# Attention with an MLP gate: one tile's statistics on ScalarE, normalization on VectorE, dummy products in the prologue, more half-unit scores

## The chip, the cores and the metric

The kernel runs on one core of a Trainium2 chip. The metric is device time in microseconds (us) of one execution; a profiled span is about 2 us shorter than the time of the same run. Each ratio compares runs on the same chip from the same batch. Single profiles can come from different chips, and their details vary by a few us between executions (the changed kernel's first exponential starts at 14.64 us in one profile and at 13.81 in another). Each experiment was timed five or six times beside eleven runs of the kernel before, and has a ratio with a 95% interval. A ratio is the mean time of one kernel's fast runs over that of the other's fast runs of the same rounds, so it is not quite the ratio of the medians quoted beside it.

## The reference, cut to what matters

```python
x  = A_x                                    # 1 x 2048 x 1024, bf16
xn = layernorm(x)                           # no learned scale or shift
# A: attention with 32 heads of 32, on xn
q, k, v = split(xn @ wqkv)
p = softmax(q @ k.T * 32 ** -0.5)           # 32 heads x 2048 x 2048 exponentials
s = merge_heads(p @ v) @ wo
# B: an MLP on xn, which normalizes once more
h = gelu_tanh(layernorm(xn) @ w1 + b1)      # hidden size 3584
g = silu(h @ w2 + b2)
out = x + s * g
```

The 134 million exponentials are ScalarE's work: 1024 instructions of 128x1024. Everything before the first of them is the prologue: load a token tile (128 tokens), take its mean and variance, normalize, transpose, project to K, Q and V.

## The kernel before, in the parts that matter

A small planner in the kernel lists all operations with estimated durations and dependencies, simulates the engines, and fixes the order of the instructions of each engine. Constants at the top steer it; a changed estimate can therefore reorder instructions anywhere. One *unit* is four heads, 256 queries and 256 keys: eight score products, two exponentials, and the P·V products. A Q block is 256 queries, and eight units (one for each pair of token tiles as keys) make up one block's row. Q products are made for 512 queries at a time; what is called Q block 1 below is the second of these, and the first unit that needs it is unit 16.

The prologue normalizes tiles and transposes them by DMA from tile 2 on; GpSimd normalizes all tiles that are not in `DN`:

```python
DN = (2, 3)
XA, XB, XW = 8, 5, 9
...
    for t in (lo, lo + 1):
        if t in DN:
            xnop[t] = dve(lambda e, t=t: e.tensor_scalar(xnb[t % 4], xst[t], mv[:, t, 0:1], lnp[:, t, 1:2],
                          op0=ALU.subtract, op1=ALU.mult), 360, [XS(t), ("mv", t), ("rs", n)], [("xnb", t % 4)], 0.5)
            continue
        xnop[t] = pool(lambda e, t=t: e.tensor_scalar(xnb[t % 4], xst[t], lnp[:, t, 1:2], lnp[:, t, 5:6], ...
    for t in (lo, lo + 1):
        ...
            add("SP", lambda e, t=t: e.dma_start_transpose(out=xnT[:, :, t * 128:(t + 1) * 128], in_=xnb[t % 4]),
                1290, 0, [("xnb", t % 4)], ...)
    pro_q.append(k_pair_item(n, False))
```

SyncE issues every transfer, in one queue (158.12 of the 160.16 MB that the page counts; the rest is listed as instructions): the transposes, and also the first MLP weights, of which the first product starts only at 65.29 us. The first w1 loads are held back to certain tiles by an extra dependency (the last argument); the w2 loads are not held back by tiles at all:

```python
def load_w1(p):
    ...
        dma(f"w1{gi}{i}", lambda e, i=i, src=src: e.dma_start(w1r[gi][:, 4 * i:4 * i + 4], src), 332000, [], [("w1", gi, i)], 3,
            [xnop[XW + 2 * p]] if p < 3 else [])

def load_w2(q, r):
    ...
    src = B_w2[r * 7 * 128:(r + 1) * 7 * 128, q * 256:(q + 1) * 256].rearrange("(f p) n -> p f n", p=128)
    dma(f"w2{i}", lambda e: e.dma_start(w2r[:, i], src), 580000, [], [("w2", i)])
```

Scores of the first `NARROW` = 16 units are issued in halves of two heads, so that an exponential can start after four products:

```python
if u < NARROW:
    for h in range(2):
        plan.s_queue.append(add("PE", lambda e, h=h: s_fn(e, (2 * h, 2 * h + 1)), 232.0, TL + 30, R, [("S", pr[h])], mode="r"))
else:
    plan.s_queue.append(add("PE", lambda e: s_fn(e, range(4)), 235.0, TL + 30, R, [("S", pr[0]), ("S", pr[1])], mode="r"))
```

The softmax here doesn't subtract the row's maximum and nothing guards it: scores larger than these inputs give would overflow.

## Time and profile before

| | before |
|---|---|
| time, median (range) | 1057.43 us (1055.95 to 1057.48), 3 runs |
| profiled span | 1055.8 us |
| ScalarE: start of first exponential | 15.25 us |
| ScalarE: gaps from there until it never waits again | 19.15 us |
| ScalarE: from the end of the last exponential to the end | 14.15 us |

ScalarE is busy without a break in the middle (930.00 of 930.00 us between 100 and 1030), so the last three rows are where time can be won: an earlier first exponential, smaller gaps after it, a shorter tail. The lines they are read from stand in the prediction. Columns: start, duration of issuing, queue, line, kind, out<-in, number of issues.

```profile
36.35 1.93 SPq L933 DMA_DIRECT2D w1r<-in_B_w_dram  x2
38.33 0.51 SPq L940 DMA_DIRECT2D w2r<-in_B_w_dram  x1
38.88 3.98 SPq L894 DMA_TRANSPOSE big<-gw  x2
```

### The profile page before, as it was taken

What the parts mean: (1) busy time and instruction counts of PE and PEld (TensorE: products, weight loads), DVE (VectorE), ACT (ScalarE), POOL (GpSimd) and SP (SyncE); (2) the same over time, 40 slices, a digit from 0 to 9 for tenths busy, and PEclk for the clock granted to TensorE, in tenths of its full rate; (3) what the DMA queues carried; (4) which work ended last, traced back from release to release, by engine and by line L of the source; (5) the groups of instructions that cost most, each with busy time, mean ns of one, the idle gap of its engine ahead of it and who ended that gap; (6) DMA issues with size and microseconds to landing.
All of it is one profiled execution on the core that took longest, in us unless ns stands there. A gap on an engine that the chain in (4) does not pass through costs nothing.

```text
span 1055.8 us, 31978 instructions
## 1 busy us (share of the span) xinstructions
PE 1024.0 (97%) x14230; PEld 632.8 (60%) x14230; DVE 967.9 (92%) x1463; ACT 1010.3 (96%) x1100; POOL 28.6 (3%) x40
## 2 busy tenths in 40 slices
PE   7998999999999999999999999999999999899997
PEld 4565457656666566656765666556665566564442
DVE  7579899999999989999999999999899999978997
ACT  2779999999999999999999999999999999999994
POOL 3600000000000000000000000000000000000000
PEclk8999999999999999999999999999999999999999
DMA  8955256634275446633565556433664687663322
GB/s 219 232 153 156 56 144 198 184 97 117 86 219 155 135 139 188 166 89 100 160 177 143 146 159 190 135 90 99 179 196 141 192 238 206 193 195 111 124 88 71
DMA packets 302371, 160.16 MB, mean 152 GB/s; under 512 B 40218, under 2 KB 293146, under 8 KB 302234
## 3 DMA queue, kind: packets, MB, share of 16 engines
q1 hardware_dynamic: 302234, 158.12, 53.3%
q8 instruction: 112, 1.84, 0.7%
q14 instruction: 25, 0.20, 0.1%
HBM read 142.35 MB, written 12.06 MB: 146 GB/s over the span
## 4 chain that ended last, share of the span: by engine, by line
ACT 88%; PE 7%; DMA 2%; DVE 2%; SPq 0%; POOL 0%; issue 0%; DVEq 0%; POOLq 0%
ACT P L1134 82%; ACT ut L995 5%; PE ps L701 5%; ACT gw L1031 1%; PE ps L696 1%; PE ps L1120 1%; DMA big<-yT 1%; DMA hT<-in_A_x_dram 1%; DVE ut L854 0%; DMA big<-gw 0%; DVE w1r L1281 0%; DVE V L771 0%; SPq L715 0%; POOL gw L886 0%; SPq L723 0%
## 5 line engine op out<-in xcount | busy, mean ns | idle before, releaser
L1134 ACT ACTIVATE P<-ps 128x1024 bf16<-128x1024 f32 x1024 | 965.3, 1245 | 23.4 <-PE ps L1120 23.3
L1164 DVE TENSOR_TENSOR PA<-P 128x2048 bf16<-128x2048 bf16 x246 | 298.7, 1216 | 15.8 <-ACT P L1134 15.1
L701 PE MATMUL ps<-yT,w1r 128*128 128x256 bf16 x1792 | 231.4, 274 | 3.4 <-DVE nv L1217 1.6
L701 PE MATMUL ps<-w2r,hT 128*128 128x256 bf16 x1792 | 227.2, 274 | 1.6 <-DVE hT L998 0.9
L701 PEld LDWEIGHTS ps<-yT,w1r 128*128 128x128 bf16 x1792 | 162.5, 98 | 58.9 <-issue 30.2
L701 PEld LDWEIGHTS ps<-w2r,hT 128*128 128x128 bf16 x1792 | 162.2, 98 | 53.0 <-issue 31.2
L696 PE MATMUL ps<-P,V 128*32 128x256 bf16 x4096 | 146.5, 274 | 0.0
L1169 DVE TENSOR_TENSOR PA<-PA 128x1024 bf16<-128x1024 bf16 x204 | 138.2, 681 | 1.5
L701 PE MATMUL ps<-big,qk 128*128 128x512 bf16 (+2 forms) x568 | 134.6, 368 | 1.5 <-DMA big<-gw 0.8
L701 PE MATMUL ps<-qk,big 128*128 128x256 bf16 (+1 forms) x736 | 127.3, 306 | 3.2 <-DMA big<-gw 2.7
L696 PEld LDWEIGHTS ps<-P,V 128*32 128x32 bf16 x4096 | 96.5, 96 | 35.6 <-issue 22.6
L1120 PE MATMUL ps<-qk 32*128 32x256 bf16 x2048 | 106.0, 273 | 8.6 <-ACT P L1134 7.6
L1120 PE MATMUL ps<-QKT 32*128 32x256 bf16 x2048 | 101.7, 273 | 2.7 <-ACT P L1134 2.3
L701 PEld LDWEIGHTS ps<-qk,big 128*128 128x128 bf16 x736 | 64.9, 98 | 45.0 <-issue 17.7
L701 PEld LDWEIGHTS ps<-big,qk 128*128 128x128 bf16 x568 | 50.5, 102 | 52.6 <-issue 16.0
L980 DVE TENSOR_TENSOR xb<-ps,b1T 128x512 bf16<-128x512 f32 x112 | 76.4, 685 | 4.7 <-PE ps L701 4.0
L1120 PEld LDWEIGHTS ps<-qk 32*128 32x128 bf16 x2048 | 31.6, 92 | 75.9 <-ACT P L1134 71.6
L1120 PEld LDWEIGHTS ps<-QKT 32*128 32x128 bf16 x2048 | 30.3, 92 | 71.5 <-ACT P L1134 68.5
L995 ACT ACTIVATE ut<-ut 128x1024 f32<-128x1024 f32 x56 | 72.5, 1295 | 0.0
L998 DVE SCALAR_TENSOR_TENSOR hT<-ut,xb 128x1024 bf16<-128x1024 f32 x56 | 67.9, 1212 | 1.3 <-ACT ut L995 1.0
L993 DVE SCALAR_TENSOR_TENSOR ut<-hT,xb 128x1024 f32<-128x1024 bf16 x56 | 68.0, 1214 | 0.0
L696 PE MATMUL ps<-PA,ones 128*32 128x256 bf16 x896 | 46.4, 275 | 0.0
(79 smaller groups left out, 529.7 us busy)
## 6 DMA issues: line engine op xcount, KB each, us to landing
w1r<-in_B_w_dram SPq DMA_DIRECT2D x224, 256.0 KB, 3.5
w2r<-in_B_w_dram SPq DMA_DIRECT2D x128, 448.0 KB, 4.3
qk<-in_A_wqkv_dram SPq DMA_DIRECT2D x16, 256.0 KB, 3.3
g_scratch<-gw SPq DMA_DIRECT2D x32, 128.0 KB, 3.6
o_scratch<-ot SPq DMA_DIRECT2D x56, 64.0 KB, 3.1
big<-o_scratch SPq DMA_DIRECT2D x28, 128.0 KB, 3.7
hT<-in_A_x_dram SPq DMA_DIRECT2D x10, 256.0 KB, 4.2
qk<-in_A_wqkv_dram SPq DMA_DIRECT2D x4, 512.0 KB, 3.7
```

The source lines that it names most:

```text
L696: ins = e.matmul(dst(j), lhsT=lhsT(j), rhs=rhs(j), start=start, stop=stop, tile_position=(0, 32 * j), skip_group_check=True)
L701: return e.matmul(dst, lhsT=lhsT, rhs=rhs, start=start, stop=stop, skip_group_check=True)
L980: dve(lambda e: e.tensor_tensor(xb_t[i2][:, p % 2].rearrange("p (k t) -> p k t", k=2), bank(it.bank).rearrange("p (k t) -> p k t", k=2), b ...
L993: dve(lambda e, r=r: e.scalar_tensor_tensor(ut_t[i2][:, r], h[:, r], 1.0 / GA, xb[:, r], op0=ALU.add, op1=ALU.mult), c_f32(r.stop - r.star ...
L995: act(lambda e: e.activation(ut_t[i2][:], ut_t[i2][:], ACT.Tanh, scale=GC * GA), c_acts(1024), [("ut", i2, 0), ("ut", i2, 1)], [("ut", i2, ...
L998: dve(lambda e, r=r: e.scalar_tensor_tensor(h[:, r], ut_t[i2][:, r], 1.0, xb[:, r], op0=ALU.add, op1=ALU.mult), c_f32(r.stop - r.start), [ ...
L1031: act(lambda e: e.activation(zh, z, ACT.Tanh, scale=0.5), c_acts(1024), [("z", 0), ("z", 1)], [("zh",)], 1)
L1120: ins = e.matmul(bank(b0[j], kk * 256, (kk + 1) * 256), lhsT=QKT[sl][32 * j:32 * j + 32, 1, kb * 128:(kb + 1) * 128], rhs=QKT[sl][32 * j:3 ...
L1134: x = act(lambda e, h=h: e.activation(P[pi][:, 2 * h:2 * h + 2].rearrange("p j k q -> p (j k q)"), ps[:, pr[h] * 1024:(pr[h] + 1) * 1024], ...
L1164: add2.append(dve(lambda e, p0=p0, a0=a0: e.tensor_tensor(PA_all[:, a0:a0 + 2].rearrange("p u j q -> p (u j) q"), P_all[:, p0:p0 + 2, :, 0 ...
L1169: add4.append(dve(lambda e, a0=a0: e.tensor_tensor(PA[a0], PA[a0], PA[a0 + 1], op=ALU.add), c_b16(1024), [("PA", a0 + 1)], [("PA", a0)], P ...
```

## The change

It means to shorten the prologue: ScalarE takes the statistics of tile 2 (two passes with a summed output) in place of VectorE; VectorE normalizes every tile in place of GpSimd; dummy products fill TensorE's idle time up to 32 us, in the hope that its clock, granted at 0.50 from 10.20 to 13.62 and from 20.44 to 23.86 us in the kernel before, stays at 1.00; 22 instead of 16 units are scored in halves; a fourth token tile is loaded ahead of the Q/K weights (`XF`). Duration estimates and constants of the planner are corrected, which reorders the rest. Core of the diff (cuts marked):

```diff
-HARD = 45
+HARD = 48
-AGE_D = 2500
-HOLD = 500
+AGE_D = 3500
+HOLD = 400
-GRACE1 = 4000
+GRACE1 = 2500
-XF = 3
+XF = 4
-DN = (2, 3)
+DN = (2, 3, 4, 5, 6, 7, 8, 9, 10, 11, 12, 13, 14, 15)
-PART = 3
+PART = 4
+HALF = 1
+NU = 22
+AS = (2,)
+FILL = 300
 ...
             if best is None:
+                if self.fill and t < 32000 and nxt > t + FILL and (t > 6000 or not self.fill[0].left):
+                    bf = bank_for(t)
+                    if bf is not None and bf[0] <= t:
+                        it = self.fill.pop()
+                        best = (t, 3, it.chunks[0], (it, bf[1]))
 ...
-    NARROW = 16
-    plan.narrow = 2 * NARROW
+    NARROW = NU
+    plan.narrow = 2 * NARROW if HALF else NARROW
 ...
+                if t in AS:
+                    junk = yT[:, 4:8, :].rearrange("p c t -> p (c t)")
+                    act(lambda e, t=t: e.activation(junk, xst[t], ACT.Copy, scale=-1.0 / 32768, accum_out=lnp[:, t, 2:3]), ...)
+                    act(lambda e, t=t: e.activation(junk, xst[t], ACT.Square, bias=lnp[:, t, 2:3], scale=1.0 / 32,
+                                                    accum_out=mv[:, t, 1:2]), ...)
+                    dve(lambda e, t=t: e.tensor_scalar_mul(mv[:, t, 0:1], lnp[:, t, 2:3], -32.0), ...)
+                else:
                     ... (BN_STATS and BN_AGGR as before)
 ...
-            if u < NARROW:
+            if u < 16:          # sums of P by TensorE: the same units as before
```

More of the change, by code (lines that the diff above doesn't have):

```diff
@@ L43 @@
 NCUT = 2
+HALF = 1
+NU = 22
+QE = 0
+AS = (2,)
+FILL = 300
+ADJ2 = 0
 TD = 2
@@ L78, in __init__ @@
         self.skip = []
+        self.fill = []
         self.ring_last = {}
@@ L117, in units_of @@
     def units_of(self, s):
+        if not self.half:
+            return s
         return s // 2 if s < self.narrow else s - self.narrow // 2
@@ L129, in run @@
         state = {"mode": "c", "bw": 0.0, "s": 0, "pv": 0, "pvopen": [], "dopen": None, "susp": None,
-                 "done": 0.0, "last_bank": 7}
+                 "done": 0.0, "cend": 0.0, "last_bank": 7}
         bank_free = {b: [] for b in (4, 5, 6, 7)}
@@ L160, in commit @@
                 state["bw"] = max(state["bw"], t) + o.nbytes / 380.0
-                o.fin = state["bw"] + {"w1": WLAT, "w2": WLAT, "tp": 2400.0, "x0": 1900.0, "x1": 1900.0}.get(o.sem[:2], 2300.0)
+                o.fin = state["bw"] + {"w1": WLAT, "w2": WLAT, "tp": 2800.0, "x0": 2050.0, "x1": 2000.0, "x2": 2500.0}.get(o.sem[:2], 2300.0)
             else:
@@ L298, in pe_step @@
                 if o.left == 0:
-                    cands.append((o.ready, 1, o, None))
+                    late = state["mode"] == "f" and state["dopen"] is not None
+                    cands.append((max(o.ready, state["cend"]) + ADJ2 if late else o.ready, 1, o, None))
             if state["dopen"] is not None:
@@ L360, in pe_step @@
             if best is None:
+                if self.fill and t < 32000 and nxt > t + FILL and (t > 6000 or not self.fill[0].left):
[3 more added lines that the diff above has]
+                        best = (t, 3, it.chunks[0], (it, bf[1]))
+            if best is None:
                 if nxt < INF:
@@ L366, in pe_step @@
             if o.mode != state["mode"]:
-                start += 95.0
+                start += 105.0 if state["mode"] == "c" else 95.0
                 state["mode"] = o.mode
@@ L386, in pe_step @@
                     state["pv"] += 1
+                elif cls == 3:
+                    o.item.k = 1
                 else:
@@ L389, in pe_step @@
                     heads[opening[2]] += 1
-            if cls == 0:
+            if cls == 3:
+                pass
+            elif cls == 0:
                 state["s"] += 1
@@ L401, in pe_step @@
                 it.k += 1
+                if cls == 1:
+                    state["cend"] = start
                 if it.k == len(it.chunks):
@@ L437, in run @@
                 wake(max(t, soon[e][0][0]), e)
+        for it in self.fill:
+            it.chunks[0].dead = True
+            it.chunks[0].start = it.chunks[0].fin = 0.0
         left = [o for o in self.ops if o.start is None]
@@ L564, in bass_recurrent_scan__mha_block__mixer_channel_mlp__prompt_kernel @@
     plan = _Plan()
-    NARROW = 16
-    plan.narrow = 2 * NARROW
+    NARROW = NU
+    plan.narrow = 2 * NARROW if HALF else NARROW
+    plan.half = HALF
     WARM = 13
@@ L722, in load_qk @@
             src = A_wqkv[:, which * D + hg * 128: which * D + (hg + 1) * 128].rearrange("(c p) n -> p c n", p=128)
-            dma(f"wqk{i}", lambda e: e.dma_start(wqk[i], src), 262144 * 8 // 5, [], [("wqk", i)], 3,
+            dma(f"wqk{i}", lambda e: e.dma_start(wqk[i], src), 262144 * 2, [], [("wqk", i)], 3,
                 [xnop[NT - 1]] if nqk["n"] == 3 else [])
@@ L728, in load_v @@
             src = A_wqkv[:, 2 * D + pr * 256: 2 * D + (pr + 1) * 256].rearrange("(c p) n -> p c n", p=128)
-            dma("wv", lambda e: e.dma_start(wv, src), 665000, [], [("wv",)])
+            dma("wv", lambda e: e.dma_start(wv, src), 850000, [], [("wv",)])
         for t in range(XF):
@@ L809, in warm_item, with fill_item @@
             return it
+        def fill_item():
+            it = _Item("fill")
+            chunk(it, lambda e, b: full(e, bank(b), ident[:], ident[:].unsqueeze(1).to_broadcast([128, 4, 128]), True, True), Q512, [("ident",)])
+            return it
         def qk_tile_item(t):
@@ L850, in bass_recurrent_scan__mha_block__mixer_channel_mlp__prompt_kernel @@
         pro_q.append(warm_item())
+        plan.fill = [fill_item() for _ in range(80)]
         for n in range(NPR):
             for t in (2 * n, 2 * n + 1):
-                for c in range(2):
-                    dve(lambda e, t=t, c=c: e.bn_stats(stats[:, t, c, :], xst[t][:, c * 512:(c + 1) * 512]),
-                        600, [XS(t)], [("st", t, c)], 1)
-                dve(lambda e, t=t: e.bn_aggr(mv[:, t, :], stats[:, t, :, :].rearrange("p c s -> p (c s)")),
-                    150, [("st", t, 0), ("st", t, 1)], [("mv", t)], 1)
+                if t in AS:
+                    junk = yT[:, 4:8, :].rearrange("p c t -> p (c t)")
+                    act(lambda e, t=t: e.activation(junk, xst[t], ACT.Copy, scale=-1.0 / 32768, accum_out=lnp[:, t, 2:3]),
+                        c_acts(1024) + 93, [XS(t)], [("yT", 2), ("yT", 3), ("st", t, 0)], 1)
+                    act(lambda e, t=t: e.activation(junk, xst[t], ACT.Square, bias=lnp[:, t, 2:3], scale=1.0 / 32,
+                                                    accum_out=mv[:, t, 1:2]),
+                        c_acts(1024) + 186, [XS(t), ("st", t, 0)], [("yT", 2), ("yT", 3), ("st", t, 1)], 1)
+                    dve(lambda e, t=t: e.tensor_scalar_mul(mv[:, t, 0:1], lnp[:, t, 2:3], -32.0), 65,
+                        [("st", t, 0), ("st", t, 1)], [("mv", t)], 1)
+                else:
+                    for c in range(2):
+                        dve(lambda e, t=t, c=c: e.bn_stats(stats[:, t, c, :], xst[t][:, c * 512:(c + 1) * 512]),
+                            600, [XS(t)], [("st", t, c)], 1)
+                    dve(lambda e, t=t: e.bn_aggr(mv[:, t, :], stats[:, t, :, :].rearrange("p c s -> p (c s)")),
+                        150, [("st", t, 0), ("st", t, 1)], [("mv", t)], 1)
                 for k in range(XA, NT):
@@ L867, in bass_recurrent_scan__mha_block__mixer_channel_mlp__prompt_kernel @@
                     dve(lambda e, t=t: e.tensor_scalar(xnb[t], xst[t], mv[:, t, 0:1], lnp[:, t, 1:2],
-                                                       op0=ALU.subtract, op1=ALU.mult), 75 + 0.26 * 1024,
+                                                       op0=ALU.subtract, op1=ALU.mult), 455,
                         [XS(t), ("mv", t), ("rs", 0, t)], [("xnb", t)], 0.5)
                 pro_q += [tr_item(0), qk_tile_item(0), tr_item(1, 0), tr_item(1, 1), qk_tile_item(1)]
+                if VLAG == 0:
+                    pro_q.append(v_item(0, 0, "pro"))
                 continue
@@ L882, in bass_recurrent_scan__mha_block__mixer_channel_mlp__prompt_kernel @@
                     xnop[t] = dve(lambda e, t=t: e.tensor_scalar(xnb[t % 4], xst[t], mv[:, t, 0:1], lnp[:, t, 1:2],
-                                                                 op0=ALU.subtract, op1=ALU.mult), 360,
+                                                                 op0=ALU.subtract, op1=ALU.mult), 455,
                                   [XS(t), ("mv", t), ("rs", n)], [("xnb", t % 4)], 0.5)
@@ L902, in bass_recurrent_scan__mha_block__mixer_channel_mlp__prompt_kernel @@
             pro_q.append(v_item(0, n, "pro"))
+        q_at = len(pro_q)
         pool(lambda e: e.tensor_tensor(lnp[:, :, 2], mv[:, :, 1], lnp[:, :, 1], op=ALU.mult), 150,
@@ L950, in make_y @@
             for i in range(2):
-                dve(lambda e, i=i: e.tensor_scalar_mul(dg[:, i, :], identf[:], lnp[:, 2 * c + i, 3:4]), 140,
+                dve(lambda e, i=i: e.tensor_scalar_mul(dg[:, i, :], identf[:], lnp[:, 2 * c + i, 3:4]), 193,
                     [("s3",), ("identf",)], [("dg", i)], 2)
@@ L1126, in unit @@
             R = [("Q", sl, qb), ("K", sl, kp)]
-            if u < NARROW:
+            if u < NARROW and HALF:
                 for h in range(2):
@@ L1151, in unit @@
             R = [("P", pi, 0), ("P", pi, 1), ("V", vs, kp)]
-            if u < NARROW:
+            if u < 16:
                 vc = add("PE", lambda e: d_fn(e, pv.bank), 4 * Q256, TL, R + [("ones",)], [], item=pv)
@@ L1213, in norm @@
             i = g % 2
-            a = dve(lambda e: e.transpose(nt_t[i][:], bank(pv.bank, 256, 512)), c_ps(256), [], [("nt", i)], 1, pv)
+            a = dve(lambda e: e.transpose(nt_t[i][:], bank(pv.bank, 256, 512)), 368, [], [("nt", i)], 1, pv)
             last = g == HG * NQB - 1
             if not last:
-                dve(lambda e: e.tensor_copy(nv_t[i][:], bank(pv.bank, 0, 256)), c_ps(256), [], [("nv", i)], 1, pv)
-            dve(lambda e: e.reciprocal(nr_t[i][:], nt_t[i][:].rearrange("p (b k) -> p b k", k=32)[:, :, 0]), 150,
+                dve(lambda e: e.tensor_copy(nv_t[i][:], bank(pv.bank, 0, 256)), 309, [], [("nv", i)], 1, pv)
+            dve(lambda e: e.reciprocal(nr_t[i][:], nt_t[i][:].rearrange("p (b k) -> p b k", k=32)[:, :, 0]), 106,
                 [("nt", i)], [("nr", i)], 2.2)
             dve(lambda e: e.transpose(nb_t[i][:].rearrange("p (b k) -> p b k", k=32),
-                                      nr_t[i][:].unsqueeze(2).to_broadcast([128, 8, 32])), c_f32(256),
+                                      nr_t[i][:].unsqueeze(2).to_broadcast([128, 8, 32])), 360,
                 [("nr", i)], [("nt", i), ("nb", i)], 2.2)
@@ L1224, in norm @@
                 return dve(lambda e: e.tensor_tensor(ot_dst, bank(pv.bank, 0, 256), nb_t[i][:], op=ALU.mult), c_ps(256),
-                           [("nb", i)], W, 1, pv, extra)
+                           [("nb", i), ("nt", i)], W, 1, pv, extra)
             return dve(lambda e: e.tensor_tensor(ot_dst, nv_t[i][:], nb_t[i][:], op=ALU.mult), c_f32(256),
-                       [("nb", i), ("nv", i)], W, 2.2, None, extra)
+                       [("nb", i), ("nv", i), ("nt", i)], W, 2.2, None, extra)
         OTr = xnT
@@ L1294, in bass_recurrent_scan__mha_block__mixer_channel_mlp__prompt_kernel @@
         for tq in range(1, 4):
-            plan.queues["proj"].append(qk_item(0, 0, tq, wq0, 16 * tq - 12))
-            plan.queues["proj"][-1].after = 1000
+            it = qk_item(0, 0, tq, wq0, 16 * tq - 12)
+            if tq == 1 and QE:
+                it.kind, it.due = "pro", 1
+                pro_q.insert(q_at - QE, it)
+                continue
+            plan.queues["proj"].append(it)
+            it.after = 1000
         for w in range(HG):
```

## The prediction

> **What bounds the kernel now.** I read the page's busy shares, its slices, the chain of work that ended last, then ScalarE's timeline, then TensorE, VectorE, GpSimd and the DMA queue over the first 66 us, then the last 16 us.
>
> ```profile
> PE 1024.0 (97%) x14230; PEld 632.8 (60%) x14230; DVE 967.9 (92%) x1463; ACT 1010.3 (96%) x1100; POOL 28.6 (3%) x40
> ACT  2779999999999999999999999999999999999994
> POOL 3600000000000000000000000000000000000000
> ACT 88%; PE 7%; DMA 2%; DVE 2%; SPq 0%; POOL 0%; issue 0%; DVEq 0%; POOLq 0%
> ```
>
> ScalarE ends 88% of the chain and is full in all slices but the first three and the last. A stretch-by-stretch table gives it 930.00 busy of 930.00 us between 100 and 1030. So the time is ScalarE's work (1010.3 us) plus its idle time (45.5 us), and only the two ends have idle time. ScalarE's timeline of the beginning lists it in brackets:
>
> ```profile
> 8.66 1.02 ACT L845 ACTIVATE big<-ps 128x1024 bf16<-128x1024 bf16 x1 [6.44 <-PE ps L834]
> 15.25 1.94 ACT L1134 ACTIVATE P<-ps 128x1024 bf16<-128x1024 f32 x2 [4.21 <-PE ps L1120]
> 24.23 7.44 ACT L1134 ACTIVATE P<-ps 128x1024 bf16<-128x1024 f32 x8 [7.05 <-PE ps L1120]
> 32.27 1.94 ACT L1134 ACTIVATE P<-ps 128x1024 bf16<-128x1024 f32 x2 [0.60 <-PE ps L1120]
> 34.88 7.53 ACT L1134 ACTIVATE P<-ps 128x1024 bf16<-128x1024 f32 x8 [0.67 <-PE ps L1120]
> 44.00 1.94 ACT L1134 ACTIVATE P<-ps 128x1024 bf16<-128x1024 f32 x2 [1.59 <-PE ps L1120]
> 46.53 1.94 ACT L1134 ACTIVATE P<-ps 128x1024 bf16<-128x1024 f32 x2 [0.60 <-PE ps L1120]
> 50.68 7.51 ACT L1134 ACTIVATE P<-ps 128x1024 bf16<-128x1024 f32 x8 [2.21 <-PE ps L1120]
> 64.61 12.94 ACT L1134 ACTIVATE P<-ps 128x1024 bf16<-128x1024 f32 x14 [6.43 <-PE ps L1120]
> ```
>
> The first exponential starts at 15.25. From there to 64.61 only 32 exponentials run, with 7.05 + 0.60 + 0.67 + 1.59 + 0.60 + 2.21 + 6.43 = **19.15 us** of gaps. Fourteen in 12.94 us, some of that overlap, make one about 0.92 us. After 64.61 ScalarE never waits until its last exponential ends at 1041.65; the tail of 14.15 us is the last P·V, the last norm, output products and stores.
>
> Why the gaps? Scores need K, K needs the transposed tokens, and those come by DMA transposes issued by SyncE from tiles that GpSimd normalizes from tile 4 on. TensorE, GpSimd and the queue's waits show the rest:
>
> ```profile
> 10.62 3.38 PE L701 MATMUL ps<-big,qk 128*128 128x128 bf16 x32
> 20.33 3.52 PE L701 MATMUL ps<-big,qk 128*128 128x256 bf16 x16 [0.23 <-DMA big<-yT]
> 34.90 1.04 PE L701 MATMUL ps<-big,qk 128*128 128x256 bf16 x8
> 35.78 2.37 POOL L886 TENSOR_SCALAR gw<-w2r,lnp 128x1024 bf16<-128x1024 bf16 x2
> SPq L894 <- POOL gw L886: 6.6, 4, 1.9
> ```
>
> Sixteen products take 3.52 us at 20.33 where eight take 1.04 us at 34.90: the first ran at half clock (granted 0.50 in the microseconds 21 and 22, and in 11 and 12). GpSimd takes 1.19 us a tile, is busy 9.46 of the 10 us from 35 to 45, and the transposes wait for it. The last tile is normalized at 41.78. From 45 to 64 TensorE is full: it is paying off V, P·V and the next Q block. The wait of 6.43 us is for unit 16, whose Q block is the last product of that backlog and is copied out at 64.03.
>
> [...]
>
> **The change, part by part**, with the order of the built instructions of both kernels beside the durations of the trace before.
>
> 1. *Tile 2's statistics on ScalarE, and x3 loaded ahead of the Q/K weights.* VectorE loses two BN_STATS of 0.64 us; ScalarE gains two passes over 128x1024, about 1.1 us each by the 1.02 us evacuation of that size, inside its 6.44 us of idle: no cost. VectorE waited for x3 until 8.78. In the new order the statistics of tiles 2 and 3 come before the second normalization; adding up durations, tiles 2 and 3 are normalized at about 11 instead of 16.1. Their K then lands near 15.5 instead of 20.3.
> 2. *Dummy products.* 29 instead of 13: 18 ahead of the first transpose, then 2, 1, 1, 6 and 1. They fill what is idle. Kept warm, the two cold bursts save 3.38/2 = 1.7 and 3.52 - 2 x 0.9 = 1.7 us. The first 1.7 brings the first exponential from 15.25 to about 13.6.
> 3. *All tiles from 4 on normalized by VectorE.* GpSimd loses 12 x 1.19 us, VectorE gains 12 x 0.46 (0.54 with overlap taken off) = 5.5 us, less 1.4 us from part 1. VectorE becomes the pacer: per pair of tiles 4 x 0.60 statistics, 2 x 0.46, about 0.35 of small ones and 0.34 + 0.60 for K and V copies, some 4.6 us. Going down its new order with these, the pairs 4-5, 6-7, ... 14-15 are normalized at about 18.7, 23, 28, 32, 37.5 and 38.5 (before: 41.8 for the last). With a median of 4.3 us from issue to landing and one transpose issued every 1.3 us, K of pairs 1 to 7 is usable at about 17.7, 25, 29, 34.5, 38.5, 43.5 and 46.5; before, the K copies ended at 22.6, 24.3 (Q), 28.6, 33.9, 36.4, 43.3, 50.0 and 52.1. Each K releases four exponentials (3.7 us; six after the first), so ScalarE's gaps are about 2.5, 1.7, 0.5, 1.6, 0.2 and 1.6: **8.1 us**.
> 4. *Half-unit scores for 22 units instead of 16, Q block 1 earlier.* In the new order that Q block's products stand ahead of K 5, 6 and 7, and the four banks of the half-unit scheme go on while P·V of the first two blocks still holds its banks. The wait of 6.43 us should vanish: 63 instead of 46 exponentials run before the first MLP tanh.
>    Check by TensorE: between the first score and the score after the MLP scale it had 49.4 us, of which 4.9 idle and 1.7 cold: 42.7 us of work. The new order adds a Q block (8 x 0.217 = 1.7 us) and 11 score issues of 0.33 us (3.6 us): 48 us. From 13.2 with 1.5 to 2.5 us of unavoidable waits that ends near 63, when some 47 exponentials must be out. 63 - 13.6 - 46.5 x 0.92 leaves 6.6 us of gaps: TensorE allows what part 3 asks for, without room to spare.
> 5. *Changed planner constants* (grace times, ages, PART 4, HOLD). They trade VectorE adds for TensorE sums: 19 fewer adds, 80 more narrow products of about 0.027 us (2.2 us of TensorE). At the end, 39 instead of 28 wide products follow the last P·V: 11 x 0.217 = **2.4 us more tail**. TensorE is in debt because ScalarE got ahead of it.
>
> Sum: 1.6 (earlier start) + 19.15 - 9 (gaps; 8.1 and about one for slips in the queue) - 2.4 (tail) = **9.4 us** from 1057.43: 1048.0. Exact ScalarE work in the middle is unchanged.
>
> **Rivals.** *TensorE becomes the bound in the middle.* It is busy 915.76 of 930 us there. Its 490 weight loads that waited for an exponential took 140.2 us, 0.286 each, and a mode change alone shows 0.21, so only about 37 us are free. Dense work now starts 17 exponentials later in ScalarE's order and at the last tanh is still 7 later (125 to go instead of 132), so it catches up about 9 us out of these. If it can't, ScalarE gets gaps it never had after 64: 1051 to 1057. For it: the longer tail. Against it: 37 exceeds 9 + 2.
> *The queue stays the pace.* DMA share was 1.0 to 1.2 from 26 to 55 us, and the weight loads still stand between the transposes. If landing, not normalizing, paced K, gaps stay near 13: 1052. Against it: 6.6 us of the queue's waits are for GpSimd's tiles.
> *VectorE becomes the bound.* 86% busy in 10 to 20 us, 89% in 26 to 35, now with 4 us more. If its copies of K slip behind, gaps of 11 us: 1050.
> *Everything fits better* (no slip, gaps of 5): 1044.
>
> **Range and chances.** The ceiling of the change is the 31.3 us of idle before 64.61, of which some 11 must stay for loads, first statistics and first transposes. A 2% gain means under 1036.3, 21 us less, which would need practically no gaps and no longer tail: 0.03. A 2% loss means over 1078.6, which a schedule with the same middle cannot reach by the terms above: 0.01. My range is 1041.0 to 1054.0: gaps of 2 to 15 us with the rest held.
>
> **What would show it.** In the new profile: first exponential at 13 to 14.5; no stretch of granted clock 0.5 between 8 and 25; GpSimd's busy time 14 us less; gaps after the first exponential of 7 to 11 instead of 19.15, none near 6 us at the change to whole units; the 47th exponential some 12 us earlier; ScalarE 100% busy from about 65 on; a tail of 16 to 17 us. I am wrong if new ScalarE gaps stand after 100 us, if transposes land 5 us and more after their tiles, or if the longer tail eats the gain.

The sum: 1.6 + 19.15 - 9 - 2.4 = 9.4 us, 1048.0. What the traces show: in the kernel before, TensorE had no product from 16.31 to 19.04 (2.73 us), and the granted clock was 0.50 from 20.44 us; a normalized tile took 0.54 us on VectorE and 1.19 on GpSimd; ScalarE loads a table once in either kernel (1.28 us).

## The result, and the profile after

| | before | after |
|---|---|---|
| time, median (range), 4 runs each | 1057.45 us (1055.95 to 1057.48) | 1056.56 us (1055.43 to 1057.32) |
| profiled span | 1055.8 us | 1055.5 us |
| first exponential | 15.25 us | 14.64 us |
| gaps after it | 19.15 us | 16.80 us |
| tail | 14.15 us | 16.29 us |

The ratio is 0.9994 [0.9977, 1.0011]: the same time. The parts add up, by the two profiles: 0.61 us from the start, 2.35 us from the gaps, less 2.14 us for the tail and 0.5 us more of ScalarE's own work in between, is the 0.3 us between the spans. Three lines of the changed kernel's page (busy times, ScalarE's slices, the chain's shares):

```profile
PE 1028.4 (97%) x14326; PEld 637.6 (60%) x14326; DVE 960.5 (91%) x1454; ACT 1013.0 (96%) x1104; POOL 14.8 (1%) x28
ACT  4699999999999999999999999999999999999993
ACT 85%; PE 11%; DMA 2%; DVE 1%; SPq 0%; issue 0%; DVEq 0%
```

GpSimd's 13.8 us are gone, and the front slices are fuller, but TensorE's share of the chain rose from 7 to 11%. ScalarE's timeline shows where it waits; the bracket is the idle time ahead of the group and what ended it:

```profile
14.64 1.94 ACT L1181 ACTIVATE P<-ps 128x1024 bf16<-128x1024 f32 x2 [3.41 <-PE ps L1167]
22.09 5.61 ACT L1181 ACTIVATE P<-ps 128x1024 bf16<-128x1024 f32 x6 [5.51 <-PE ps L1167]
...
38.66 3.77 ACT L1181 ACTIVATE P<-ps 128x1024 bf16<-128x1024 f32 x4 [2.53 <-PE ps L1167]
44.35 1.94 ACT L1181 ACTIVATE P<-ps 128x1024 bf16<-128x1024 f32 x2 [1.92 <-PE ps L1167]
49.11 1.02 ACT L1181 ACTIVATE P<-ps 128x1024 bf16<-128x1024 f32 x1 [2.83 <-PE ps L1167]
...
54.61 1.02 ACT L1181 ACTIVATE P<-ps 128x1024 bf16<-128x1024 f32 x1 [1.46 <-PE ps L1167]
...
58.30 22.26 ACT L1181 ACTIVATE P<-ps 128x1024 bf16<-128x1024 f32 x24 [0.56 <-PE ps L1167]
```

The old wait of 6.43 us at unit 16 is gone. New ones stand at 49 to 55: one exponential at a time. TensorE's timeline of the same moment, and below it, in a table of stretches, the granted clock (the third number from the end of a row, ahead of DMA share and GB/s):

```profile
47.91 0.62 PE L728 MATMUL ps<-big,qk 128*128 128x256 bf16 x4 [2.83 <-DMA big<-gw]
49.01 1.03 PE L728 MATMUL ps<-big,qk 128*128 128x256 bf16 x4
```

```profile
46.00:48.00 2.00, 0.09 (x1) 0.09 (x2) 0.48 (x2) 0.28 (x1) 0.38 (x1) 1.00 1.23 276
50.00:52.00 2.00, 2.00 (x13) 0.66 (x12) 1.05 (x2) 1.16 (x2) 0.00 (x0) 0.50 0.86 249
```

TensorE stood idle for 2.83 us waiting for a transposed tile (the pair 12 and 13), with the DMA engines full (share 1.23 from 46 to 48). Then the clock fell to 0.50: four K products take 1.03 us instead of 0.61. The DMA queue at that time:

```profile
37.85 1.13 SPq L980 DMA_DIRECT2D w1r<-in_B_w_dram  x2
39.02 0.52 SPq L987 DMA_DIRECT2D w2r<-in_B_w_dram  x1
40.32 6.93 SPq L940 DMA_TRANSPOSE big<-gw  x3
```

Issuing three transposes took 6.93 us, and the view of this line in 40.0 to 41.9 gives the landing of the first of them, tile 12:

```profile
L940 SPq DMA_TRANSPOSE big<-gw x1: 2027/2027/2027, 40.3 to 40.3; - x1
DMA to landing us min/median/max: 6.6/6.6/6.6
```

Tile 13, issued at 42.4, took 5.5 us and landed at 47.9, which is when TensorE went on. VectorE had normalized both tiles by 40.75, so it was not what TensorE waited for. The w2 load issued ahead of them took 7.0 us and landed at 46.04; tile 12 landed 0.9 us behind it.

All of these transfers go through SyncE's one queue, and tile 12 landed just after the load issued ahead of it. So the transposes may have stood behind a w2 load of 448 KB that the kernel does not need until much later (its first MLP product, on w1, starts at 75.21). That is a theory so far; this profile does not show that the load held them up.

### The profile page after: what moved, and what is told of

The parts are those of the page before. It is cut to its first block, busy times and chain, and to the rows that moved or that the text cites. A ratio compares the mean times of both kernels' runs of the same rounds, so it can differ in the third digit from the quotient of the medians.

```text
span 1055.5 us, 32143 instructions
## 1 busy us (share of the span) xinstructions
PE 1028.4 (97%) x14326; PEld 637.6 (60%) x14326; DVE 960.5 (91%) x1454; ACT 1013.0 (96%) x1104; POOL 14.8 (1%) x28
## 4 chain that ended last, share of the span: by engine, by line
ACT 85%; PE 11%; DMA 2%; DVE 1%; SPq 0%; issue 0%; DVEq 0%
ACT P L1181 79%; PE ps L728 7%; ACT ut L1042 5%; PE ps L723 2%; PE ps L1167 2%; ACT gw L1078 1%; DMA big<-gw 1%; DMA big<-yT 1%; DMA hT<-in_A_x_dram 0%; DVE w1r L1328 0%; DVE ut L898 0%; SPq L742 0%; PE ps L866 0%; DVE V L1331 0%; DVE V L1328 0%
## 5 line engine op out<-in xcount | busy, mean ns | idle before, releaser
L1216 DVE TENSOR_TENSOR PA<-PA 128x1024 bf16<-128x1024 bf16 x201 | 135.6, 681 | 1.2
L1167 PE MATMUL ps<-qk 32*128 32x256 bf16 x2048 | 108.6, 274 | 6.0 <-ACT P L1181 5.4
L728 PEld LDWEIGHTS ps<-big,qk 128*128 128x128 bf16 x568 | 47.8, 98 | 57.4 <-issue 17.3
L1261 DVE STREAM_TRANSPOSE nt<-ps 128x256 f32<-128x256 f32 x64 | 28.6, 446 | 22.8 <-PE ps L723 22.6
```

Source lines behind the costliest of these rows:

```text
L728: return e.matmul(dst, lhsT=lhsT, rhs=rhs, start=start, stop=stop, skip_group_check=True)
L1167: ins = e.matmul(bank(b0[j], kk * 256, (kk + 1) * 256), lhsT=QKT[sl][32 * j:32 * j + 32, 1, kb * 128:(kb + 1) * 128], rhs=QKT[sl][32 * j:3 ...
L1216: add4.append(dve(lambda e, a0=a0: e.tensor_tensor(PA[a0], PA[a0], PA[a0 + 1], op=ALU.add), c_b16(1024), [("PA", a0 + 1)], [("PA", a0)], P ...
L1261: a = dve(lambda e: e.transpose(nt_t[i][:], bank(pv.bank, 256, 512)), 368, [], [("nt", i)], 1, pv)
```

## The experiments

**The theory (Q, the queue):** late landing behind weight loads, with the half clock that follows, ate the gain; loads moved behind the last transposes give it back. **Rival B:** TensorE is near its limit, and what ScalarE gains at the start comes back as waits or as a longer tail. **Rival C:** the dummy products or the early loads of x tiles are the harm. **Rival D:** what is left of the gain is due to one part alone.

### 1. Weight loads behind the transposes (hold_after), in the changed kernel

```diff
-                    [xnop[XW + 2 * p]] if p < 3 else [])
+                    [xnop[NT - 1]] if p < 3 else [])
-            dma(f"w2{i}", lambda e: e.dma_start(w2r[:, i], src), 580000, [], [("w2", i)])
+            dma(f"w2{i}", lambda e: e.dma_start(w2r[:, i], src), 580000, [], [("w2", i)], 3, [xnop[NT - 1]] if nw2["n"] <= NW2R else [])
```

In the trace the instructions of VectorE, ScalarE and GpSimd come in the order of the changed kernel, and those of TensorE too but for some missing records; only the DMA queue differs, with the transposes of tiles 8 to 15 ahead of all these weights.

> The changed kernel with its first MLP weight loads held back until the last token tile is normalized; every engine but the DMA queue keeps its order. Theory A (late transposes): the transposes of tiles 12 to 15, which took 5.5 to 6.6 us to land behind three weight loads, land in about 3 to 4; TensorE's idle 2.83 us at 45 to 48 goes below 1, the half clock from 48 to 55 is gone, ScalarE's gaps after its first exponential fall from 16.8 to 11 to 13, and the time falls by 3 to 5 us to about 1052. Theory B (the end belongs to TensorE): the gaps fall the same way but the tail after the last exponential grows by as much, and the time falls by under 1 us. Theory C (the queue itself is slow): landing stays at 5 to 6 us and nothing changes.

Measured: 1050.65 us (1050.01 to 1050.87) beside 1058.15 for the kernel before, ratio 0.9928 [0.9914, 0.9942]. ScalarE's timeline of this run:

```profile
13.50 1.94 ACT L1181 ACTIVATE P<-ps 128x1024 bf16<-128x1024 f32 x2 [2.56 <-PE ps L1167]
20.34 5.61 ACT L1181 ACTIVATE P<-ps 128x1024 bf16<-128x1024 f32 x6 [4.90 <-PE ps L1167]
...
42.41 4.69 ACT L1181 ACTIVATE P<-ps 128x1024 bf16<-128x1024 f32 x5 [1.92 <-PE ps L1167]
...
50.78 29.60 ACT L1181 ACTIVATE P<-ps 128x1024 bf16<-128x1024 f32 x32 [0.52 <-PE ps L1167]
```

Its DMA queue, with the landing of two of the transposes (39.7 and 41.1), and one stretch of its table:

```profile
38.38 4.03 SPq L940 DMA_TRANSPOSE big<-gw  x3
DMA to landing us min/median/max: 2.8/2.8/2.8
```

```profile
48.00:50.00 2.00, 2.00 (x21) 1.30 (x18) 0.32 (x1) 2.00 (x3) 0.00 (x0) 1.00 0.79 197
```

The same transposes land in 2.7 and 2.8 us, the clock stays at 1.00, and of the waits that stood between 46 and 58 (5.98 us) 0.83 us are left: gaps of 10.84 us in all. The last exponential ends at 1031.90 of a span of 1048.2, 7.3 us earlier than in the changed kernel, and all of it reaches the end: the tail is 16.3 us as before. So Q holds, with a gain somewhat above the 3 to 5 us expected, and rival B, which wants the gain to come back later, does not.

### 2. One w2 load alone (holdw2)

Only the second of the two edits above. In effect a single load of 448 KB moves from just ahead of the transposes of tiles 12 to 15 to after them; the other w2 loads were behind them already, and the w1 loads stay where they were.

> A smaller dose: of the loads ahead of the transposes of tiles 12 to 15 only the w2 loads (448 KB each) are held back; the w1 loads stay where the changed kernel has them. Theory A: the transpose of tile 12 lands in 4 to 5.5 us instead of 6.6 (2.8 with all held back), and the time lies between the changed kernel (1057) and the held-back one (1050.5): 1051 to 1055. Rival: only some other effect of the reordering counts, then it equals one of the two.

Measured: 1049.74 us (1049.35 to 1052.29), before 1058.41, ratio 0.9923 [0.9909, 0.9938]. Its queue:

```profile
36.81 1.13 SPq L980 DMA_DIRECT2D w1r<-in_B_w_dram  x2
39.26 4.60 SPq L940 DMA_TRANSPOSE big<-gw  x3
```

and TensorE at the wait that was 2.83 us:

```profile
44.38 0.61 PE L728 MATMUL ps<-big,qk 128*128 128x256 bf16 x4 [0.35 <-DMA big<-gw]
```

The transposes land in 4.1, 3.8 and 2.9 us, the gaps are 11.42 us, and TensorE, VectorE, ScalarE and GpSimd run in the order of the changed kernel. The expectation that this would bring only a part was a miss: the two edits cannot be told apart. One transfer, a 350th part of the kernel's 160 MB, carried the loss as far as these runs can tell.

### 3. The changed kernel again (after_again)

No edit: this asks whether the half clock is there in every execution.

> The changed kernel itself beside the others of this call. Expected: 0 to 0.3% under the kernel before (about 1056), with a spread of 3 us and more between its runs, because after the 3 us in which TensorE waits for tile 13 the clock falls to half in some runs and for different lengths (theory A). If the spread comes from something else, the profile shows full clock from 45 to 58 and the same time.

Measured: 1056.98 us, before 1058.06, ratio 0.9983 [0.9965, 1.0000], but its runs fall into two groups, each with its own mean granted clock:

| run | 1 | 2 | 3 | 4 | 5 | 6 |
|---|---|---|---|---|---|---|
| us | 1053.46 | 1057.36 | 1058.47 | 1056.62 | 1053.35 | 1057.33 |
| clock | 0.999 | 0.992 | 0.992 | 0.993 | 0.999 | 0.993 |

The profile fell on run 1. TensorE's timeline there:

```profile
46.96 0.61 PE L728 MATMUL ps<-big,qk 128*128 128x256 bf16 x4 [2.85 <-DMA big<-gw]
47.83 0.61 PE L728 MATMUL ps<-big,qk 128*128 128x256 bf16 x4
```

The same idle stretch, 2.85 us, yet the clock stayed at 1.00 (in every stretch of the table from 44 to 58). So in these two runs it was not the length of the wait that decided, and what does is not shown. The last microseconds of a run left out, half clock lasted 3.41 us twice in the kernel before (10.20 to 13.62 and 20.44 to 23.86), 6.83 us in the first profile of the changed kernel (48.38 to 55.20) and 13.7 us in that of nofill_after (45.2 to 58.9). Here are the 3.41 us just ahead of the fall in the first profile, with 0.57 us of work for TensorE:

```profile
44.97:48.38 3.41, 0.57 (x5) 0.31 (x4) 0.48 (x2) 1.31 (x2) 1.41 (x1) 1.00 0.87 196
```

The run at full clock splits the 7.3 us between the spans of the changed kernel (1055.5) and the held one (1048.2). From the wait for tile 13 on, the gaps are 5.98 us with the half clock, 3.42 without it in this run, and 0.83 with the loads held: 2.6 us are the half clock's and 2.6 us the late landing's own. The other 0.8 us of gaps and 1.1 us in the start of the first exponential (14.64 against 13.50) come ahead of the moved loads and vary between executions (first exponentials at 12.64 to 14.64 in the profiles of the changed kernel's variants). holdw2, with nearly the start and early gaps of this run, confirms the 2.6 us: 1049.1 against 1051.7. The table of runs gives the clock more: its four low runs average 1057.4 us, its two high ones 1053.4, so 4 us. At 0.992 the half clock presumably lasted longer than in the first profile: there a mean of 0.995 went with 6.8 us of it, and in the profile of nofill_after (below) 0.992 with 13.7. Over all timed runs of the changed kernel, eight of ten had a mean clock of 0.992 to 0.995; all twelve of the two held versions above had 0.998 or 0.999, and in their two profiles the clock does not fall before the last microseconds.

### 4. The dummy products (nofill_after, hold_nofill)

```diff
-FILL = 300
+FILL = 10**9
```

This takes out the 16 dummy products that the change added; every other instruction keeps its order. Tried on the changed kernel and on the held one.

> The changed kernel without its 16 added dummy products; every other instruction in the same order. Theory A: half clock is back in 10 to 13 and 20 to 23, the first exponential comes 1 to 1.6 us later and K of pair 1 about 1.5 us later; time 1 to 3 us longer. Rival: those stretches wait for transfers anyway, the time stays within 0.5 us.

> The kernel with held-back weight loads, without the 16 added dummy products, all else in the same order. If dummies are worth their two cold bursts: half clock again in 10 to 13 and 20 to 23 us, time 1.5 to 3 us above the held-back kernel (1050.65 in the call before). Rival: the waits of that stretch end by transfers, the difference is within 0.7 us.

Measured on the changed kernel: 1053.43 us (1050.90 to 1057.51), ratio 0.9960 [0.9940, 0.9979]; its runs spread over 6.6 us, and the profiled one, at 1057.51, has half clock from 45.2 to 58.9. So it is not slower without them, and it suffers from the same late landing. The half clock expected in 10 to 13 and 20 to 23 us is not in this profile at all: the clock is 1.00 up to 45.2. On the held kernel, where the spread is small: 1049.72 us (1048.80 to 1051.27), before 1058.06, ratio 0.9926 [0.9911, 0.9941], against 0.9928 with them. One of its stretches shows the clock that the dummies were meant to save:

```profile
10.00:12.00 2.00, 2.00 (x21) 2.00 (x20) 1.51 (x4) 0.29 (x1) 0.00 (x0) 0.50 1.11 350
```

The first burst of half clock is back (9.1 to 12.6 us; the second, at 20 to 23, is not), and the first exponential starts at 14.06 instead of 13.50; but the next group starts at 19.89 instead of 20.34. That group needs K of the first transposed pair, and in the held kernel the chain into it runs 5.86 us through the landing of a transposed tile, which no product can hasten; here that tile landed in 4.1 us instead of 5.9. No gain from the dummies can be told from zero; the two intervals leave room for some 2 us either way.

### 5. The early x loads (xb3_after, hold_xb3)

In the changed kernel the transposes of tiles 2 and 3 go out 4 us earlier than before (11.62 and 13.02 instead of 15.69 and 17.09), but right behind loads of x tiles 8 and 9, and take 5.7 and 6.7 us to land instead of 3.3 and 3.2. This edit puts those loads behind them.

```diff
-XB = 5
+XB = 3
```

> The changed kernel with the loads of token tiles 8 and 9 behind the first two transposes instead of ahead of them. Theory A: these two transposes land in about 4 us instead of 5.7 and 6.7, K of pair 1 is there near 17.5 instead of 19.8, ScalarE's wait of 5.5 us falls to about 3, part of which comes back as later waits; time 0 to 2 us shorter. Rival (queue itself slow): landing unchanged, no change.

> Both of the two above. Theory A: gaps of 9 to 11 us and a time of about 1050; theory B: gaps as small, a tail of 20 us and a time above 1055.

Measured on the changed kernel: 1056.70 us, ratio 0.9985 [0.9968, 1.0002]; on the held kernel 1050.23 us (1049.36 to 1051.05), ratio 0.9924 [0.9911, 0.9937], against 0.9928 without. The two transposes land in 3.3 and 4.5 us, and the wait ahead of the second group of exponentials shrinks from 5.51 to 4.48 us; but the next wait grows from 0.62 to 1.43, presumably because the later tiles were loaded later. No gain can be told from zero. (The planner also moves a few of VectorE's instructions with this edit.)

### 6. Is holding the loads enough alone? (hold_before)

The edit of experiment 1 in the kernel before; the planner moves some 50 rows of TensorE's order as well.

> The kernel before, with the same loads held back (its planner then reorders some 50 rows of TensorE's prologue). If the loads alone were what cost the time: 4 us and more faster than before. If normalization on GpSimd paced it, as the prediction says: K 6 and 7 come at most 1 to 2 us earlier and the time falls by 0 to 2 us.

Measured: 1056.79 us (1055.72 to 1058.35), before 1058.06, ratio 0.9993 [0.9979, 1.0007]. No gain in time, but a miss in the mechanism: K of pairs 6 and 7 was copied out at 46.7 and 47.6 us, 3.3 and 4.5 us earlier than before, although GpSimd still normalized the tiles. So the loads delayed K in the kernel before as well. The wait ahead of unit 16, where the scores change from halves to whole units, stays and takes up what was gained ahead of it; unit 16 needs Q block 1, which was copied out at 64.4 us (64.1 before).

```profile
64.86 12.94 ACT L1134 ACTIVATE P<-ps 128x1024 bf16<-128x1024 f32 x14 [7.29 <-PE ps L1120]
```

So the gain of the held kernel is not the edit's alone: the change by itself gains 0 to 0.2%, the held loads by themselves 0.1% or nothing, both together 0.7%.

### 7. Which parts of the change does the gain need? (hold_nu16, hold_gp, hold_nostat, hold_oldconst)

Each keeps the held loads and takes back one part:

```diff
 hold_nu16
-NU = 22
+NU = 16
 hold_gp
-DN = (2, 3, 4, 5, 6, 7, 8, 9, 10, 11, 12, 13, 14, 15)
+DN = (2, 3)
 hold_nostat
-AS = (2,)
+AS = ()
 hold_oldconst
-HARD, AGE_D, HOLD, GRACE1, PART = 48, 3500, 400, 2500, 4    (five lines, put on one here)
+HARD, AGE_D, HOLD, GRACE1, PART = 45, 2500, 500, 4000, 3
```

> The held-back kernel with half-unit scores for 16 units again instead of 22. If part 4 of the prediction is right: a wait of 6 to 8 us is back at the change to whole units, and the time is 5 to 8 us longer than the held-back kernel (1056 to 1058). Rival: that Q block comes early anyway, and the wait and the loss are under 2 us.

> The held-back kernel with tiles 4 to 15 normalized on GpSimd again (1.19 us a tile). If VectorE's share is what makes the gain possible (part 3): K 5 to 7 later by 2 us and more, a wait of 5 us and more before unit 16, and 4 to 8 us lost against the held-back kernel (1055 to 1058). Rival: with the loads out of the way the transposes are early enough from GpSimd too, under 2 us lost.

> The held-back kernel with tile 2's statistics on VectorE again. If part 1 matters: the first transposes are issued at 14 to 16 instead of 11.6, K of pair 1 comes 1 to 3 us later; the planner then also leaves Q block 1 late, so a wait of some 6 us before unit 16 may come back: 1055 to 1058. Rival: the first pair is held up by loads anyway, and nothing is lost.

> The held-back kernel with the old planner constants (HARD, AGE_D, HOLD, GRACE1, PART 3). The prologue's order is the same, so its gaps stay near 11 us. If PART and the other constants made the longer tail: tail back to 14 us and about 2 us faster than the held-back kernel. Rival: the tail stays at 16 us and the time within 1.5 us of it.

| | median us | ratio to before |
|---|---|---|
| hold_after, for comparison | 1050.65 | 0.9928 [0.9914, 0.9942] |
| hold_nu16 | 1057.98 | 1.0004 [0.9989, 1.0018] |
| hold_gp | 1059.99 | 1.0016 [0.9999, 1.0032] |
| hold_nostat | 1060.83 | 1.0023 [1.0009, 1.0037] |
| hold_oldconst | 1050.69 | 0.9928 [0.9914, 0.9942] |

The planner's new constants play no part. Taking back any of the other three loses all of the gain (the 9 to 10 us of hold_gp and hold_nostat are more than expected). ScalarE's timelines say where, one line for each of the three kernels in the order of the table:

```profile
61.48 1.94 ACT L1182 ACTIVATE P<-ps 128x1024 bf16<-128x1024 f32 x2 [6.89 <-PE ps L1168]
```

```profile
60.90 13.86 ACT L1182 ACTIVATE P<-ps 128x1024 bf16<-128x1024 f32 x15 [7.83 <-PE ps L1168]
```

```profile
61.57 13.86 ACT L1181 ACTIVATE P<-ps 128x1024 bf16<-128x1024 f32 x15 [6.74 <-PE ps L1167]
```

The same wait as in the kernel before, at the same place: ahead of unit 16, after 32 exponentials. In hold_gp and hold_nostat units 16 to 21 are still scored in halves, and their scores wait for Q block 1, which the planner again puts last; in hold_nu16 unit 16 is the first whole unit, and TensorE's row ahead of its scores says 0.72 us for the copy that frees a P·V bank. When the copies of Q block 1 and of K ended:

| us | Q block 1 | K 5 | K 6 | K 7 | wait ahead of unit 16 |
|---|---|---|---|---|---|
| hold_after | 34.5 | 41.7 | 45.3 | 50.1 | none |
| hold_nu16 | 34.6 | 41.8 | 45.3 | 50.2 | 6.89 |
| hold_gp | 60.4 | 41.4 | 43.3 | 47.2 | 7.83 |
| hold_nostat | 61.1 | 41.5 | 45.6 | 48.9 | 6.74 |
| hold_before | 64.4 | 41.1 | 46.7 | 47.6 | 7.29 |

So hold_gp was a miss in the mechanism: with GpSimd normalizing, K 5 to 7 came not 2 us later but up to 3 us earlier, and late tiles are not what brings the wait back. What goes with its absence is two things at once: Q block 1 early in TensorE's order, and the half-unit scheme for more than 16 units. Each edit makes the planner reorder the products around Q block 1, so these are not clean measurements of single parts. Untested is the obvious rival that only the order matters: Q block 1 put early by hand, with 22 half units but without the VectorE and ScalarE parts. With that reservation rival D falls: taking back any one of three parts lost the whole gain.

### 8. The tail

The tail was predicted to grow by 2.4 us because TensorE would be in debt to a ScalarE that had got ahead. It did grow by 2.1 us, but not because of the lead. The last exponential and the span of four kernels:

| | last exponential ends | span | tail |
|---|---|---|---|
| changed kernel | 1039.21 | 1055.5 | 16.3 |
| held loads | 1031.90 | 1048.2 | 16.3 |
| held loads, half units 16: the lead is lost | 1039.33 | 1055.3 | 16.0 |
| held loads, old constants | 1033.61 | 1049.9 | 16.3 |

For the changed kernel this is read from the last group of ScalarE's timeline (1019.51 + 19.70), in the stretch 1020 to 1056:

```profile
1019.51 19.70 ACT L1181 ACTIVATE P<-ps 128x1024 bf16<-128x1024 f32 x21
```

Seven microseconds more or less of lead move the tail by 0.3. It is a property of the order that the planner makes for this kernel: the traces show 28 wide products (128x512) after the last P·V before and 39 after, as the prediction counted. The old constants do not undo the longer tail, and which of the other changes makes the planner put more products there stays open.

The best versions, hold_nofill (1049.72), holdw2 (1049.74) and hold_xb3 (1050.23), cannot be told apart; all beat the kernel before by about 0.75% and the changed one by about 0.6%. For use I would take holdw2, the smallest edit.

## Why the prediction was wrong

The bound was read rightly: ScalarE's work plus its idle time at the two ends, and nothing new in the middle (929.93 us busy of 930 between 100 and 1030). Of the sum's terms:

- **Earlier start, predicted 1.6 us.** Measured 0.61 us in the profile of the changed kernel, 1.44 and 1.75 us in those of after_again and hold_after. The term lies within what the start varies by, and the clock was 1.00 from 8 to 25 us as said. (Ahead of 7.4 us the trace holds no clock record, and a 1.00 of its tables means nothing there: the dummy products came every 0.43 us up to then and every 0.22 us after.) What the dummies were worth was not borne out: no loss without them can be told from zero (experiment 4).
- **GpSimd's part moved to VectorE.** GpSimd lost 13.8 us, as said. That this brings K earlier is not shown: with the loads held, K 5 to 7 came at least as early from GpSimd (experiment 7). In the held kernel tiles 12 and 13 are normalized by 38.8 us (predicted 37.5); tiles 14 and 15 by 40.9, where 38.5 was predicted.
- **The wait of 6.43 us at unit 16.** Predicted to vanish; it did, and no other longer than 6 us took its place. Part 4 named the two conditions, Q block 1 early and half units beyond 16, and experiment 7 shows the wait wherever one of them is missing.
- **Gaps of 9 us: the step that failed.** It is this sentence of part 3: "With a median of 4.3 us from issue to landing and one transpose issued every 1.3 us, K of pairs 1 to 7 is usable at about 17.7, 25, 29, 34.5, 38.5, 43.5 and 46.5". A median over the kernel before was used for transposes whose place in the queue was known: behind a w2 load. (In the kernel before, too, tiles 10 to 12, behind weight loads, took over 5 us where tiles 8 and 9 took 3.2 and 2.9.) The one pair that mattered took 6.6 and 5.5 us, and issuing slowed from 1.3 to 2.0 and 3.5 us a transpose. K of pair 6 was copied out at 50.5 instead of 43.5. The allowance "about one for slips in the queue" should have been larger by 2.6 us for this landing, by 2.6 us of half clock, which no term had, and by 2.6 us for what lies ahead of it: 16.8 instead of 9. With the load out of the way the pair lands in 2.8 us, K 6 is copied out at 45.3, and the gaps are 10.84 us. The misses ahead of it are two, against smaller waits than said in between. The wait ahead of the second group was 5.51 us (4.90 with the loads held) where 2.5 was said, since the first transposes also took over 5 us to land. The wait ahead of pair 5 was 1.92 where 0.2 was said: in the held kernel its tiles had landed by 36.7, but TensorE worked without a break on products ordered ahead and began its K only at 40.23.
- **Tail, predicted 2.4 us longer.** The size was right (2.1), and so was the count of products behind it; the reason given for them ("TensorE is in debt because ScalarE got ahead of it") was not (experiment 8).
- **The rivals.** "The queue stays the pace" was the right one. The prediction had even put down that "the weight loads still stand between the transposes" and set it aside because 6.6 us of the queue's waits before were for GpSimd. That argument was wrong already in the kernel before: with the loads held and GpSimd as slow as ever, K of pairs 6 and 7 came 3.3 and 4.5 us earlier (experiment 6). The rival's estimate of 1052 lies near the runs that kept their clock (1053.4); the half clock makes the other 4 us of most runs. "TensorE becomes the bound" is rejected by experiment 1. "VectorE becomes the bound" does not explain the loss: the tiles were ready at 40.75, later than the 37.5 said, but TensorE waited for their landing at 47.9.

With the queue in order the kernel takes 1049.7 to 1050.7 us, inside the predicted range. So the sum of the terms was about right without that load, and the miss is the term for what the change ran into. The fit is partly luck: in the held kernel two waits were 2.4 and 1.7 us longer than said, and others shorter (0.62 for 1.7 at pair 2, 0.83 for 1.6 at pair 6).

## What to carry to other kernels

When a change makes the producer of a transfer faster, look at the queue's order at the new time of issue, not at the median landing before: list what stands ahead of the critical transfer and ask what of it could come later. Here the transposes of tiles 12 and 13 landed in 2.7 and 2.8 us with no weight load ahead of them (hold_after), in 4.1 and 3.8 behind two w1 loads (holdw2), and in 6.6 and 5.5 when a w2 load of 448 KB was added (changed kernel), where issuing them took 2.0 and 3.5 instead of 1.3 us. The price varied: behind the same three loads they took 5.1 and 3.6 us in the kernel before. Moving that w2 load was worth 6 to 7 us of 1057 (ratio 0.9923 against 0.9983). A wait of 2.83 us on TensorE was followed by half clock that cost another 2.6 us, and only in some runs (eight of ten had the low mean clock), so read the granted clock of every run and not of the profiled one alone. Before filling an idle TensorE, check whether the stretch that follows is limited by TensorE or by an arrival; here 16 dummy products gained nothing that can be told from zero (ratio 0.9928 with them, 0.9926 without). And where a planner reorders a kernel after every edit, compare the order itself between runs before crediting a part of the change with a gain.
